# Fused retention and two MoE-style layers on one core: an early load of the first weight half, short tiles moved in the order of tiles, and their values loaded by two queues

## The chip, the cores and the metric

The kernel runs on one core of a Trainium2 chip. The metric is device time in microseconds (us) of one execution, as the median of several runs; lower is better. The trace shown is one execution, taken by the hardware profiler. Engines are PE (TensorE), DVE (VectorE), ACT (ScalarE), POOL (GpSimd) and SP (SyncE, which here only issues DMAs). ACT also issues DMAs, on a queue of its own.

## What is computed

Causal retention over 4 batches, 8 heads, 576 tokens and 64 channels a head, then two dense layers over the 2304 tokens, each with a weight into 2048 features, an elementwise function and a weight back to 512:

```python
scores = scale * np.matmul(q, k.transpose(0, 1, 3, 2))
gamma = 1.0 - 2.0 ** (-5.0 - np.arange(H, dtype=np.float32))
Dmat = np.where(rel >= 0, gamma[:, None, None] ** rel[None, :, :], 0.0)
x = np.matmul(scores * Dmat[None], v)          # then to (tokens, 512)
h = x @ w_in;   x = np.square(np.maximum(h, 0.0)) @ w_out
h = x @ w_in2;  out = (h * np.clip(h + 3.0, 0.0, 6.0) / 6.0) @ w_out2
```

All is float32; the weights come as 64-bit words that the kernel turns into float32 itself.

## The kernel before

**Retention, first 65 us.** The 576 tokens of a batch are cut into four full tiles of 128 and one short tile of 64. Batches are worked in pairs (0 and 1, then 2 and 3), and the list `tiles` (L199) holds 20 entries: for a pair, tile 0 of both batches, tile 1 of both, and so on, the two short tiles last. For tile `ti` the loop at the end of the file writes `stage_scores(ti)` (L302, matmuls `aps`; DVE multiplies them by a decay into `ret`, L310), then, for the tile before, `values(ti - 1)`: `stage_values` (L349, matmuls `vps` from `ret` and the values in `kvt`), `stage_state` (L325, `sps`, full tiles only), `stage_queries` (L361, into `vps` again, from the second tile of a batch on), DVE's copy into `xall` (L369) and ACT's copy of the state (L336, four instructions, full tiles only). POOL scales the keys of a full tile in place (L278). So PE's order for a full tile is scores of the next one, values, state, queries; a short tile has no state.

**Loads.** A full tile has two DMAs of 512 KB on SP: `qk` (L243) and `kv` (L257). Two short tiles of a pair form one unit: two DMAs of 256 KB for `qk` on SP (L248), and for the values two DMAs of 256 KB, one for each half of the partitions, both issued by ACT (L261). The first eight units are loaded at the start; the others as space comes free, from inside `values`. Eight semaphores are handed round to all DMAs of both queues in turn, so a DMA is issued when the one eight before it has landed, and an instruction behind it on its engine waits with it.

**Weights.** A weight half (chunk `c` of 128 features, `which` 0 for `w_in`, 1 for `w_out`) is loaded by `load_w` (for `w_in` of the first layer four DMAs, L137 to L141, in pieces of 1 KB; `w_out` one DMA, L145), then decoded: two ACT instructions (L165, L166), then DVE's (L169, L172, L178, L184), then `split_to` makes a high part on ACT (L190) and a low part on DVE or POOL (L191). The list `halves` is the order: (-2) `w_in` 0, (-2) `w_in` 1, (-1) `w_in` 2, (-1) `w_out` 0, then the rest. Before the change `w_in` 0 is loaded at `ti` 9 and `w_in` 1 at `ti` 13 (inside `values`), and five further halves at `ti` 14 to 18. `w_in` 0 is decoded from `ti` 14 on, `w_in` 1 after the last tile, `w_in` 2 and `w_out` 0 after the first chunk of the layer has been issued to PE.

**First layer.** For chunk `i`, `emit_h` issues 24 matmuls (`hps`, L434: 512 and 256 columns wide) into two banks that are the same for every one of the first 16 chunks; `emit_g` evacuates them with ACT (L454 to L456 on 512 columns, then on 256) and DVE (L460); `y_steps` of chunk `i - 2` follow (`yps`, L477). So the first three chunks, h0, h1 and h2, run with no `y` between them, and each needs the evacuation of the one before.

Of the kernel before, what the change touches and what calls it, by code (L numbers as in the profile page):

```python
# [24 lines left out]
C = 128  # L25
# [45 lines left out]
def retention_moe_moe2(ctx, tc, qk, qk_last, kv, w_in, w_out, w_in2, w_out2, consts, out):  # L71
# [127 lines left out]
    tiles = [(b, i, min(C, S - C * i)) for pair in range(0, B, 2) for i in range(NTB) for b in (pair, pair + 1)]  # L199
    data, rets, held = {}, {}, {}  # L200
# [22 lines left out]
    FULL = 2 * TILES  # L223
    UNITS = (FULL + 1) * (B // 2)

# [11 lines left out]
    def load_qk(u):  # L237
        p, i = divmod(u, FULL + 1)
        held[u] = spaces(u)
        first = (FULL + 2) * p + i  # L240
        if i < FULL:
            b, i, n = tiles[first]
            nc.sync.dma_start(out=held[u][0], in_=qk[b, i])  # L243
            data[first] = [held[u][0].rearrange("p (e a t) -> p e a t", e=2, a=HP)]
            return
        t = held[u][0].rearrange("p (b f) -> p b f", b=2)
        for k in range(2):
            nc.sync.dma_start(out=t[:, k], in_=qk_last[2 * p + k])  # L248
            data[first + k] = [t[:, k].rearrange("p (e a t) -> p e a t", e=2, a=HP)]

    def load_kv(u):
        p, i = divmod(u, FULL + 1)
        first = (FULL + 2) * p + i
        t = held.pop(u)[1].rearrange("p (e h d) -> p e h d", e=2, h=H)
        if i < FULL:
            b, i, n = tiles[first]
            nc.sync.dma_start(out=t, in_=kv[b, C * i:C * i + n])  # L257
            data[first] += [t[:, 0], t[:, 1]]
# [6 lines left out]
        for k in range(2):  # L265
            data[first + k] += [None, t[:, k]]
# [465 lines left out]
    with tc.manual_schedule():  # L732
# [6 lines left out]
        rows = place("t3", [128, C_END - C_GQ], F32, "rows")  # L739
# [3 lines left out]
        load_kv(1)  # L743
        for u in range(2, len(TOKENS) + WIDE):
            load_unit(u)
# [5 lines left out]
        def values(ti):  # L751
# [4 lines left out]
            u = ti // (FULL + 2) * (FULL + 1) + min(ti % (FULL + 2), FULL)  # L756
            if ti % (FULL + 2) == FULL:
                return
            if u < len(TOKENS):
                load_unit(u + len(TOKENS) + WIDE)  # L760
            elif len(TOKENS) + WIDE <= u < UNITS - len(TOKENS):
                load_unit(u + len(TOKENS))
            if ti in (9, 13):
# [6 lines left out]
        for ti in range(len(tiles)):  # L770
# [41 lines left out]
        due = [decode(*halves.pop(0)[1:])]  # L812
        due[0].pop(0)()
        for i, (pos, c) in enumerate(units):
            h = emit_h(pos, c)
            if i == 0:
                third_in, first_out = due.pop(0), decode(*halves.pop(0)[1:])
                third_in.pop(0)()
                split_in(0, 1, nc.vector)
                first_out.pop(0)()  # L820
                for f in third_in:
                    f()
                next_load()
                first_out.pop(0)()
                split_in(0, 2, nc.vector)
                for f in first_out:
                    f()
                next_load()
            dec, due = due, []
            for d in dec[:1]:  # L830
# [3 lines left out]
            for d in dec[1:]:  # L834
# [6 lines left out]
            for d in dec[1:]:  # L841
# [7 lines left out]
            if i and i + 2 < len(units):  # L849
# [127 lines left out]
```

## Time and profile before

| | |
|---|---|
| median of 3 runs | 850.76 us (849.04 to 851.12) |
| profiled execution, its own time | 849.55 us |
| its span | 847.8 us |
| PE busy in the span | 834.7 us (98%) |
| mean granted TensorE clock | 0.997 of full speed |
| DMA, mean over the span | 217 GB/s |

PE is nearly always busy, so the page's busy shares say little about one stage. The timeline names for each instruction the idle time before it and what ended that idle time; the chain of waits follows the end of the program back from step to step; the DMA view gives, for a stretch, what each queue moved. q1 is SP's data queue, q10 is ACT's, q8 and q14 bring instructions.

### The profile page before, as it was taken

Reading aid. Unit: us, or ns where it says so; the run is one execution under the profiler, and the core shown is the slowest. Engines: PE = TensorE matmul, PEld = TensorE weight load, DVE = VectorE, ACT = ScalarE, POOL = GpSimd, SP = SyncE. Lnnn points to the kernel's source line nnn. Section 1 sums busy time; section 2 is a strip of 40 time slices with the busy share of each in tenths; the row PEclk is TensorE's granted clock in tenths of the full one; section 3 lists DMA queues with packets and bytes.
Section 4 is the critical chain, followed back from the end, with each engine's and each line's share of the span. In section 5 each row is a group of like instructions: output and inputs, shape, how many; then the busy total and the mean of one; then the engine's idle time right before and its main releaser. Section 6 shows DMA issues by size and latency. Waiting matters only on the chain.

```text
span 847.8 us, 13400 instructions
## 1 busy us (share of the span) xinstructions
PE 834.7 (98%) x4964; PEld 724.2 (85%) x4964; DVE 526.4 (62%) x899; ACT 460.3 (54%) x879; POOL 134.9 (16%) x114
## 2 busy tenths in 40 slices
PE   8898999999999999999999999999999999999997
PEld 7887888888888888888888898989888898889886
DVE  5688777785676777787665544546654545634433
ACT  2248776776677777787765433344433335433332
POOL 3321333331332333242230000000000000000000
PEclk9999999999999999999999999999999999999999
DMA  9993656565678768876777464462764552864521
GB/s 335 354 308 109 187 190 183 191 190 198 215 270 302 258 243 277 307 262 242 268 245 264 165 222 185 151 226 95 277 256 163 176 210 87 308 225 162 202 97 74
DMA packets 67700, 183.95 MB, mean 217 GB/s; under 512 B 6834, under 2 KB 23346, under 8 KB 67636
## 3 DMA queue, kind: packets, MB, share of 16 engines
q1 hardware_dynamic: 66480, 181.17, 60.8%
q10 hardware_dynamic: 1156, 1.94, 0.8%
q8 instruction: 39, 0.64, 0.3%
q14 instruction: 25, 0.20, 0.1%
HBM read 146.90 MB, written 36.18 MB: 216 GB/s over the span
## 4 chain that ended last, share of the span: by engine, by line
PE 94%; DMA 4%; SPq 1%; DVE 0%; issue 0%; ACT 0%; ACTq 0%; DVEq 0%
PE yps L618 24%; PE hps L434 23%; PE yps L477 21%; PE hps L652 21%; PE ytail L477 3%; DMA early<-in_qk_dram 1%; PE aps L302 1%; PE vps L349 1%; DMA qkt<-in_qk_last_dram 1%; DMA qkt<-in_qk_dram 1%; PE vps L361 0%; PE sps L325 0%; DMA stage<-in_w_in_dram 0%; DVE w L184 0%; DVE a L178 0%
## 5 line engine op out<-in xcount | busy, mean ns | idle before, releaser
L618 PE MATMUL yps<-wo,g 128*128 128x512 f32 x864 | 226.4, 394 | 0.0
L477 PE MATMUL yps<-g,wo 128*128 128x512 f32 x768 | 195.3, 392 | 0.0
L618 PEld LDWEIGHTS yps<-wo,g 128*128 128x128 f32 x864 | 159.5, 188 | 23.9 <-DVE g L667 0.3
L477 PEld LDWEIGHTS yps<-g,wo 128*128 128x128 f32 x768 | 140.0, 188 | 27.5 <-POOL wo L191 3.1
L434 PE MATMUL hps<-xring,win 128*128 128x512 f32 (+1 forms) x720 | 155.0, 364 | 2.5 <-ACT r L454 2.5
L434 PEld LDWEIGHTS hps<-xring,win 128*128 128x128 f32 x720 | 124.3, 190 | 24.1 <-ACT r L454 2.7
L652 PE MATMUL hps<-xlast,win 128*128 128x384 f32 x576 | 116.1, 336 | 0.0
L652 PEld LDWEIGHTS hps<-xlast,win 128*128 128x128 f32 x576 | 103.2, 188 | 8.8
L671 DVE TENSOR_TENSOR u<-hps,u 128x384 f32<-128x384 f32 x48 | 26.8, 558 | 107.3 <-PE hps L652 107.3
L460 DVE TENSOR_TENSOR g<-r,g 128x512 fp32r<-128x512 f32 x64 | 47.6, 743 | 70.9 <-ACT g L456 70.5
L652 PE MATMUL hps<-xop,win 128*128 128x384 f32 x432 | 87.2, 336 | 0.0
L454 ACT ACTIVATE r<-hps 128x512 f32<-128x512 f32 x80 | 44.0, 549 | 73.9 <-PE hps L434 73.9
L665 ACT ACTIVATE g<-c 128x384 fp32r<-128x384 f32 x72 | 37.9, 526 | 84.3 <-DVE c L664 84.3
L652 PEld LDWEIGHTS hps<-xop,win 128*128 128x128 f32 x432 | 77.5, 188 | 6.6
L663 ACT ACTIVATE v<-c,three 128x384 f32<-128x384 f32 x72 | 44.5, 618 | 32.9 <-DVE c L671 31.6
L434 PE MATMUL hps<-xown,win 128*128 128x512 f32 x240 | 59.8, 390 | 0.7 <-ACT xall L486 0.7
L190 ACT ACTIVATE win<-w 128x512 fp32r<-128x512 f32 x64 | 39.7, 620 | 27.1 <-DVE w L184 27.1
L434 PEld LDWEIGHTS hps<-xown,win 128*128 128x128 f32 x240 | 44.8, 188 | 10.1 <-ACT xall L486 0.9
L690 ACT ACTIVATE c<-hps 128x384 f32<-128x384 f32 x24 | 11.8, 492 | 76.4 <-PE hps L652 76.4
L169 DVE TENSOR_SCALAR a<-a 128x512 f32<-128x512 f32 x64 | 38.5, 602 | 23.6 <-ACT a L165 23.6
L455 ACT ACTIVATE r<-r 128x512 f32<-128x512 f32 x80 | 47.2, 590 | 2.5
L664 DVE SCALAR_TENSOR_TENSOR c<-v,c 128x384 f32<-128x384 f32 x72 | 40.0, 555 | 13.7 <-ACT v L663 13.7
(90 smaller groups left out, 990.1 us busy)
## 6 DMA issues: line engine op xcount, KB each, us to landing
wo<-kept SPq DMA_DIRECT2D x96, 512.0 KB, 5.1
win<-kept SPq DMA_DIRECT2D x72, 512.0 KB, 3.6
kept<-ready SPq DMA_DIRECT2D x40, 512.0 KB, 3.7
stage<-in_w_out_dram SPq DMA_DIRECT2D x32, 512.0 KB, 4.1
kept<-wo SPq DMA_DIRECT2D x16, 512.0 KB, 5.0
stage<-in_w_in_dram SPq DMA_DIRECT2D x16, 512.0 KB, 4.0
qkt<-in_qk_dram SPq DMA_DIRECT2D x13, 512.0 KB, 6.9
kvt<-in_kv_dram SPq DMA_DIRECT2D x13, 512.0 KB, 7.9
```

Source lines behind the costliest of these rows:

```text
L169: nc.vector.tensor_scalar(out=a, in0=a, scalar1=LEAST, scalar2=MOST, op0=ALU.max, op1=ALU.min)
L190: lambda: nc.scalar.activation(out=hi, in_=src, func=ACTF.Copy),
L434: nc.tensor.matmul(out=h, lhsT=w[:, wp, kk * 128:kk * 128 + 128], rhs=xs[pos, kk][xp][:, o:o + n], start=m == 0, stop=m == 3 * KD - 1,)
L454: nc.scalar.activation(out=r, in_=hs[k], func=ACTF.Relu)
L455: nc.scalar.activation(out=r, in_=r, func=ACTF.Square)
L460: nc.vector.tensor_tensor(out=lo, in0=src, in1=hi.bitcast(F32), op=ALU.subtract)
L477: nc.tensor.matmul(out=p, lhsT=w[:, wp, m * 128:m * 128 + 128], rhs=g[pos, c][k][:, gpart, :size], start=c == 0 and e == 0 and not (k and ...
L618: nc.tensor.matmul(out=p, lhsT=gt[m // 3][:, gpart, m % 3 * 128:][:, :128], rhs=w[:, wp], start=first and e == 0, stop=last and e == 2,)
L652: nc.tensor.matmul(out=to, lhsT=wl[k][:, half, wp, o], rhs=x[:, xp, f], start=first and m == 0, stop=last and m == 5, skip_group_check=True,)
L663: nc.scalar.activation(out=v, in_=c, func=ACTF.Relu, bias=three)
L664: nc.vector.scalar_tensor_tensor(out=c, in0=v, scalar=6.0, in1=c, op0=ALU.min, op1=ALU.mult)
L665: nc.scalar.activation(out=hi, in_=c, func=ACTF.Copy)
```

## The change

- `load()` for `w_in` 0 is issued on SP right behind the loads of the first two tiles.
- The two short tiles of batches 0 and 1 move behind the first full tiles of batches 2 and 3; `groups` replaces the arithmetic on unit numbers. The short tiles of batches 2 and 3 stay last.
- Of the values of short tiles, the first half goes on SP with the other loads of the unit; the second half stays on ACT's queue, but is issued at `ti` 9 and `ti` 17.
- `w_in` 1 is loaded after tile 11, and is decoded from `ti` 16 on. `w_in` 0 is decoded from `ti` 2 on and split at `ti` 6; `w_in` 1 is split at the last tile. The block that was put into chunk 0 (`third_in`, `first_out`) is gone: `w_in` 2 and `w_out` 0 are decoded as any others, and `w_in` 2 is split after `emit_g` of chunk 0, low part on POOL.
- The constants' row tile `rows` moves from `t3` to `t6`, since `t3` now takes `w_in` 0.

```diff
-    tiles = [(b, i, min(C, S - C * i)) for pair in range(0, B, 2) for i in range(NTB) for b in (pair, pair + 1)]
-    data, rets, held = {}, {}, {}
+    steps = [(p, i) for p in range(B // 2) for i in range(TILES)]
+    for p in range(B // 2):
+        at = steps.index((p + 1, 0)) + 1 if 2 * p + 2 < B else len(steps)
+        steps.insert(at, (p, TILES))
+    tiles = [(2 * p + e, i, min(C, S - C * i)) for p, i in steps for e in range(2)]
+    groups = []
+    for ti, (b, i, n) in enumerate(tiles):
+        if n == C or b % 2 == 0:
+            groups.append((ti,) if n == C else (ti, ti + 1))
+    data, rets, held, other_half = {}, {}, {}, []
...
-        for e in range(2):
-            nc.scalar.dma_start(
+
+        def part(e, queue):
+            queue.dma_start(
                 out=t[half(e)].rearrange("p b h d -> p b (h d)"),
-                in_=kv[2 * p:2 * p + 2, C * TILES:, 1].rearrange("b t h d -> t b (h d)"),
+                in_=kv[b:b + 2, C * i:, 1].rearrange("b t h d -> t b (h d)"),
             )
-        for k in range(2):
-            data[first + k] += [None, t[:, k]]
+
+        part(0, nc.sync)
+        other_half.append(lambda: part(1, nc.scalar))
+        for k, ti in enumerate(groups[u]):
+            data[ti] += [None, t[:, k]]
...
-        rows = place("t3", [128, C_END - C_GQ], F32, "rows")
+        rows = place("t6", [128, C_END - C_GQ], F32, "rows")
         nc.scalar.dma_start(out=rows[:2], in_=consts[:2, C_GQ:])
         load = lambda: load_w(*coming.pop(0)[1:])
         load_kv(0)
         load_kv(1)
+        load()
...
-            if ti in (9, 13):
+            if ti == 11:
                 load()
...
             if len(tiles) - 6 <= ti < len(tiles) - 1:
                 load()
+            if ti in (9, 17):
+                other_half.pop()()
...
-            if 9 <= ti < 9 + KD:
-                high, low = split_x(0, ti - 9)
+            if 11 <= ti < 11 + KD:
+                high, low = split_x(0, ti - 11)
...
-            if ti == 14:
+            if ti in (2, 16):
                 decoding = decode(*halves.pop(0)[1:])
                 decoding.pop(0)()
-            if ti == 18:
+            if ti == 6:
                 split_in(0, 0, nc.gpsimd)
...
-        second_in = decode(*halves.pop(0)[1:])
-        second_in.pop(0)()
+            if ti == len(tiles) - 1:
+                split_in(0, 1, nc.gpsimd)
         values(len(tiles) - 1)
-        for f in second_in:
-            f()
-        next_load()
...
-        due = [decode(*halves.pop(0)[1:])]
-        due[0].pop(0)()
+        due = [decode(*halves.pop(0)[1:]) for _ in range(2)]
+        for d in due:
+            d.pop(0)()
...
-            if i == 0:
-                third_in, first_out = due.pop(0), decode(*halves.pop(0)[1:])
...
-                split_in(0, 2, nc.vector)
...
-            if i and i + 2 < len(units):
+            if i + 2 < len(units):
                 split_in(*units[i + 2], nc.gpsimd if i + 2 < NCH else nc.vector)
```

In the fences below each row is one instruction (or "xN" equal ones) as the engine gets it; the line numbers of the changed kernel are a few higher.

**First place: SP at the start of the program.** Before:

```order
L243 DMA qkt<-in_qk_dram 128x1024 x2
L257 DMA kvt<-in_kv_dram 128x1024 x2
L243 DMA qkt<-in_qk_dram 128x1024
L257 DMA kvt<-in_kv_dram 128x1024
L243 DMA qkt<-in_qk_dram 128x1024
L257 DMA kvt<-in_kv_dram 128x1024
```

and after the change:

```order
L246 DMA qkt<-in_qk_dram 128x1024 x2
L258 DMA kvt<-in_kv_dram 128x1024 x2
L137 DMA stage<-in_w_in_dram 128x2x128
L139 DMA stage<-in_w_in_dram 128x128
L140 DMA stage<-in_w_in_dram 64x128
L141 DMA stage<-in_w_in_dram 64x128
L246 DMA qkt<-in_qk_dram 128x1024
L258 DMA kvt<-in_kv_dram 128x1024
```

The four DMAs of `w_in` 0 stand ahead of the loads of the third tile and of all that follow.

**Second place: PE and ACT around the short tiles of batches 0 and 1, after the change.** PE, from the scores of tile 9 (a full one) on; `64x64` marks a short tile:

```order
L307 MATMUL aps<-qkt 128x128 x8
L354 MATMUL vps<-ret,kvt 64x128 x8
L330 MATMUL sps<-kvt 64x64 x8
L307 MATMUL aps<-qkt 64x64 x8
L354 MATMUL vps<-ret,kvt 64x128 x8
L330 MATMUL sps<-kvt 64x64 x8
L307 MATMUL aps<-qkt 64x64 x8
L354 MATMUL vps<-ret,kvt 64x64 x8
L366 MATMUL vps<-qkt,state 64x64 x8
```

ACT, from the first tiles on; the 12 state copies ahead of the DMA are those of tiles 6, 7 and 8, the four behind it those of tile 9:

```order
L341 ACTIVATE state<-sps,cst 128x64 x8
L165 ACTIVATE a<-stage 128x512
L166 ACTIVATE r<-stage 128x512
L341 ACTIVATE state<-sps,cst 128x64 x16
L190 ACTIVATE win<-w_255 128x512
L341 ACTIVATE state<-sps,cst 128x64 x12
L263 DMA kvt<-in_kv_dram 64x2x512
L341 ACTIVATE state<-sps,cst 128x64 x4
```

ACT before the change:

```order
L796 ACTIVATE cst<-gps 128x512
L336 ACTIVATE state<-sps,cst 128x64 x4
L261 DMA kvt<-in_kv_dram 64x2x512 x2
L336 ACTIVATE state<-sps,cst 128x64 x28
L190 ACTIVATE xring<-xall 128x768 x2
```

Both ACT loads stood behind the state copies of tile 0; the one that is left stands behind those of tile 8, and PE uses what it loads in the second `vps` row of a short tile (the row `L354 ... 64x64`), five rows of PE after the state of tile 8 (the first `sps` row).

**Third place: ACT between retention and the second evacuation.** After the change, from the high part of `w_in` 1 on:

```order
L190 ACTIVATE win<-w_255 128x512
L165 ACTIVATE a<-stage 128x512
L166 ACTIVATE r<-stage 128x512
L165 ACTIVATE a<-stage 128x512
L166 ACTIVATE r<-stage 128x512
L459 ACTIVATE r<-hps 128x512
L460 ACTIVATE r<-r 128x512
L461 ACTIVATE g<-r 128x512
L459 ACTIVATE r<-hps 128x256
L460 ACTIVATE r<-r 128x256
L461 ACTIVATE gtail<-r 128x256
L190 ACTIVATE win<-w_1093 128x512
```

Then come one high part (`wo`), two decode instructions and the evacuation of h1. Before the change:

```order
L190 ACTIVATE win<-w_822 128x512
L165 ACTIVATE a<-stage 128x512
L166 ACTIVATE r<-stage 128x512
L165 ACTIVATE a<-stage 128x512
L166 ACTIVATE r<-stage 128x512
L190 ACTIVATE win<-w_822 128x512
L165 ACTIVATE a<-stage 128x512
L166 ACTIVATE r<-stage 128x512
L190 ACTIVATE win<-w_1090 128x512
L454 ACTIVATE r<-hps 128x512
```

The first evacuation (`r<-hps`) stood behind the high parts of `w_in` 1 and `w_in` 2, which wait for DVE; now it stands behind four decode instructions only, and the high part of `w_in` 2 comes behind it.

## Rows read from the trace of the kernel before

**Rows 1.** Page, part 1: busy us, share of the span, instructions by engine

```profile
PE 834.7 (98%) x4964; PEld 724.2 (85%) x4964; DVE 526.4 (62%) x899; ACT 460.3 (54%) x879; POOL 134.9 (16%) x114
```

**Rows 2.** Waits of PE, 0 to 110 us: us in total, times, longest

```profile
PE vps L349 <- issue: 1.7, 1, 1.7
PE vps L349 <- DVE xall L369: 0.5, 1, 0.5
```

**Rows 3.** Timeline, start: start us, us, engine, operation, idle before and releaser

```profile
10.65 1.16 PE L302 MATMUL aps<-qkt 64*128 64x128 f32 x16
10.85 0.69 ACTq L261 DMA_DIRECT2D kvt<-in_kv_dram  x1
11.40 1.04 POOL L278 TENSOR_TENSOR kvt<-kvt,cst 128x512 f32<-128x512 f32 x1 [1.52 <-DMA kvt<-in_kv_dram]
...
13.96 1.04 POOL L278 TENSOR_TENSOR kvt<-kvt,cst 128x512 f32<-128x512 f32 x1 [1.52 <-DMA kvt<-in_kv_dram]
...
21.62 1.16 PE L302 MATMUL aps<-early 64*128 64x128 f32 x16 [1.96 <-DMA early<-in_qk_dram]
```

**Rows 4.** Chain of waits in order of time: start us, us on the chain, what

```profile
24.86 1.09 PE aps L302 x16
25.96 1.02 PE vps L349 x16
26.98 0.46 PE sps L325 x16
27.45 0.60 PE vps L361 x16
...
34.33 0.39 PE aps L302 x14
...
38.69 0.23 PE vps L361 x16
...
86.12 4.18 PE hps L434 x24
```

**Rows 5.** DMA view, 35 to 39 us: packets, MB, share of 16 engines

```profile
q8 instruction: 1, 0.02, 1.7%
```

**Rows 6.** DMA view, 58.2 to 61 us (a `w_in` half in flight)

```profile
q1 hardware_dynamic: 854, 0.79, 105.2%
```

**Rows 7.** DMA view, 11.6 to 14.3 us: the only data queue with packets

```profile
q1 hardware_dynamic: 304, 1.11, 102.3%
```

**Rows 8.** DMA view, 14.5 to 20 us

```profile
q10 hardware_dynamic: 279, 0.52, 33.0%
```

**Rows 9.** Line L261, the four ACT loads of short values, from issue to landing

```profile
DMA to landing us min/median/max: 8.3/8.6/10.1
```

**Rows 10.** Page, part 6: KB each, median us from issue to landing

```profile
win<-kept SPq DMA_DIRECT2D x72, 512.0 KB, 3.6
```

**Rows 11.** Timeline, end of retention to the first layer

```profile
62.69 0.27 PE L349 MATMUL vps<-ret,kvt 64*64 64x64 f32 x2
...
64.76 4.45 PE L434 MATMUL hps<-xring,win 128*128 128x512 f32 x24
...
71.70 10.21 PE L434 MATMUL hps<-xring,win 128*128 128x512 f32 x48 [2.50 <-ACT r L454]
...
81.75 0.86 PE L477 MATMUL yps<-g,wo 128*128 128x512 f32 x3
```

**Rows 12.** Busy time by stretch: us, engines busy, PEclk (granted clock), DMA share, GB/s

```profile
71.70:75.40 3.70, 3.70 (x9) 2.94 (x10) 3.21 (x7) 3.60 (x8) 0.00 (x0) 0.54 0.02 4
```

**Rows 13.** Groups by form, 0 to 85 us: busy us, mean ns, idle before

```profile
L165 ACT ACTIVATE a<-stage 128x512 f32<-128x512 f32 x7 | 4.7, 670 | 0.6 <-issue 0.6
...
L184 DVE CUSTOM_DVE_ANT_0 w<-a,r 128x1024 uint16<-128x1024 uint16 x4 | 2.8, 690 | 0.3
...
L190 ACT ACTIVATE win<-w 128x512 fp32r<-128x512 f32 x4 | 2.5, 632 | 3.0 <-DVE w L184 3.0
...
L454 ACT ACTIVATE r<-hps 128x512 f32<-128x512 f32 x3 | 1.8, 587 | 0.5 <-PE hps L434 0.5
```

More of the change, by code (lines that the diff above doesn't have):

```diff
@@ L221, in make_last_decay @@
             )
-    FULL = 2 * TILES
-    UNITS = (FULL + 1) * (B // 2)
     wide = []
@@ L237, in load_qk @@
     def load_qk(u):
[L238 removed]
         held[u] = spaces(u)
[L240 to L242 removed]
+        b, i, n = tiles[groups[u][0]]
+        if n == C:
             nc.sync.dma_start(out=held[u][0], in_=qk[b, i])
[L244 removed]
+            data[groups[u][0]] = [held[u][0].rearrange("p (e a t) -> p e a t", e=2, a=HP)]
             return
         t = held[u][0].rearrange("p (b f) -> p b f", b=2)
[L247 to L249 removed]
+        for k, ti in enumerate(groups[u]):
+            nc.sync.dma_start(out=t[:, k], in_=qk_last[b + k])
+            data[ti] = [t[:, k].rearrange("p (e a t) -> p e a t", e=2, a=HP)]
     def load_kv(u):
[L252 to L253 removed]
+        b, i, n = tiles[groups[u][0]]
         t = held.pop(u)[1].rearrange("p (e h d) -> p e h d", e=2, h=H)
[L255 to L256 removed]
+        if n == C:
             nc.sync.dma_start(out=t, in_=kv[b, C * i:C * i + n])
[L258 removed]
+            data[groups[u][0]] += [t[:, 0], t[:, 1]]
             return
[L260 to L261 removed]
+        def part(e, queue):
+            queue.dma_start(
                 out=t[half(e)].rearrange("p b h d -> p b (h d)"),
[L263 removed]
+                in_=kv[b:b + 2, C * i:, 1].rearrange("b t h d -> t b (h d)"),
             )
[L265 to L266 removed]
+        part(0, nc.sync)
+        other_half.append(lambda: part(1, nc.scalar))
+        for k, ti in enumerate(groups[u]):
+            data[ti] += [None, t[:, k]]
     def load_unit(u):
@@ L755, in values @@
             stage_state_copy(ti)
-            u = ti // (FULL + 2) * (FULL + 1) + min(ti % (FULL + 2), FULL)
-            if ti % (FULL + 2) == FULL:
+            u = next(u for u, g in enumerate(groups) if ti in g)
+            if ti != groups[u][-1]:
                 return
@@ L811, in retention_moe_moe2 @@
         sums, highs, lows = operand_steps(0)
-        due = [decode(*halves.pop(0)[1:])]
-        due[0].pop(0)()
+        due = [decode(*halves.pop(0)[1:]) for _ in range(2)]
+        for d in due:
+            d.pop(0)()
         for i, (pos, c) in enumerate(units):
             h = emit_h(pos, c)
-            if i == 0:
-                third_in, first_out = due.pop(0), decode(*halves.pop(0)[1:])
[L818 to L824, printed above, removed]
-                split_in(0, 2, nc.vector)
-                for f in first_out:
-                    f()
-                next_load()
             dec, due = due, []
-            for d in dec[:1]:
+            first = dec if i == 0 else dec[:1]
+            dec = dec[len(first):]
+            for d in first:
                 for f in d:
@@ L833, in retention_moe_moe2 @@
                 next_load()
-            for d in dec[1:]:
+            for d in dec:
                 d.pop(0)()
@@ L840, in retention_moe_moe2 @@
             emit_g(pos, c, h)
-            for d in dec[1:]:
+            for d in dec:
                 for f in d:
```

2 lines of the change are left out of this document (1 added, 1 removed).

## The prediction

> **What bounds the kernel now.** I read the page first: PE is busy 834.7 of 847.8 us [rows 1], so only idle PE and PE at the lower clock can be won or lost. The waits of PE and the timeline then show where it idles in the first 85 us: 1.96 us before the scores of the sixth tile, which wait for a load [rows 3]; 0.5 us and 1.7 us around the first short tiles [rows 2]; and 2.50 us between h0 and h1, ended by ACT's evacuation [rows 11]. After that last gap the granted clock is 0.54 of full over 3.7 us [rows 12], that is the 1.2 GHz level for some 3.4 us, and h1 with h2 take 10.21 us [rows 11] where two later chunks take 2 x 4.18 [rows 4]: 1.85 us more. From the first `y` step at 81.75 on [rows 11] the work is the same in both kernels and PE-bound. So the forecast is the shift of that moment. The last values of retention that two kernels can be compared by are the first short tile's of batches 2 and 3, at 62.69 [rows 11]; from there to the `y` step before the change are 19.06 us.
>
> **Step 1, the early half.** `w_in` 0 comes in front of the third tile. At full rate a 512 KB DMA takes 1.28 us: one tile is two of them, and the keys of two tiles start 2.56 us apart [rows 3]. In 1 KB pieces the queue moved 0.79 MB in 2.8 us [rows 6], so 0.52 MB is 1.86 us; bounds 1.28 and 2.1, I take 1.86. The third tile's keys started on landing at 11.40, its first DMA one place earlier at about 10.1 [rows 3]; both come 1.86 later, so its scores start at 12.0, not 10.65. From there PE goes on without waiting: a tile is 1.09 + 1.02 + 0.46 + 0.60 = 3.17 us, 2.57 without queries [rows 4], so the sixth tile's scores start at 12.0 + 2.57 + 2 x 3.17 = 20.9. Its load would land near 13.9 + 1.86 + 3 x 1.28 = 19.6: in front of it the two ACT loads are gone, which had stretched those three DMAs from 3.84 to 7.6 us (13.9 to 21.5) [rows 3]. Instead of 21.62 it is 20.9: **-0.7**. DVE's and ACT's decode of this half moves to a place where the same engines have the same work a tile; I cost it at nothing, as it cost PE nothing at tiles 14 to 17; without that cover it is four DVE steps of at most 0.7 each [rows 13].
>
> **Step 2, the short tiles in another place.** The 0.5 us (PE was ahead of DVE's copy) and the 1.7 us with no releaser [rows 2] belonged to two short tiles behind each other. In the second, one 16 KB transfer of instructions falls in the stretch [rows 5]; I read it as PE short of instructions, because short tiles use them up fastest. Now full-width work lies between the short scores, the same number of instructions takes some 1.4 us longer (0.39 for short scores against 1.09, twice [rows 4]), and I keep 0.3 of the 2.2: **-1.9**; bounds -2.2 and 0. The Trainium skill ("Runtime: NRT & Kernel Launch", Instruction fetch mechanics) has the crossing of such a block mostly hidden; by that the gap has another cause and may stay, and the sum would be 1.7 higher. The 1.70 us in the trace speaks against "hidden" here.
>
> **Step 3, the second half of the first short values.** This is the new wait. ACT's load was issued at 10.85, just after the first state [rows 3], and used 23 us later. Now it is issued after the state of tile 8, and PE gets to its use after short scores, values, state, short scores: 0.39 + 1.02 + 0.46 + 0.39 = 2.26 us [rows 4], 2.4 with what is left of the 0.5. The four such loads took at least 8.3 us to land [rows 9]. The nearest for below are SP's loads in quiet stretches, 3.6 us for twice the bytes [rows 10]. Here the queue is not quiet: SP issues its loads until the semaphore ring stops it, eight DMAs ahead. Before, in 11.6 to 14.3 only SP's queue had packets, though ACT's load had been issued at 10.85 [rows 3, 7]; in 14.5 to 20 both ACT loads passed, 0.52 MB in 5.5 us [rows 8]. So: about 3.4 us before the first packet, 2.75 for one load, 0.4 for the last engine: 6.6 from issue, nearest to the 8.3 row but with one load instead of two. State 8 ends 5.74 us after the scores of tile 8 begin (two scores, two values, two states, one queries). Those begin three tiles of 3.17 after the sixth, at 30.4; so issue 36.2, landing 42.8, use at 38.5: **+4.3**; bounds +1.0 and +5.9. Queued behind on PE is everything; behind on SP the reload of that unit's space, which has five tiles of slack.
>
> A gap that long is beyond the 2.50 us after which the clock fell, while 1.96 and 1.70 did not lower it. So the clock falls: **+1.5** (1.85 was the price in wide matmuls).
>
> **Step 4, the second half of the last short values.** Issue after state 16, use after queries, short scores, a full values-state-queries, short scores: 0.60 + 0.39 + 1.02 + 0.46 + 0.60 + 0.39 = 3.46, less 0.1. On SP the five weight halves are in flight then, mostly landed; I take 5.4 us: **+2.0**; bounds 0.2 and 5.2.
>
> **Step 5, the first layer's start.** From the values of the first last short tile the path is now ACT's: short matmuls, DVE's copy and last decode step (about 1.8 us, L184 0.69 [rows 13]); then sixteen ACT instructions up to and with the evacuation of h1, thirteen at 0.59 to 0.67 and three half as wide, 9.5 us [rows 13]; then h2, 4.18 [rows 4]. That is 15.5, with latencies 15.8, against 19.06: **-3.3**. Below stands the path of PE alone, 1.0 + 3 x 4.18 = 13.5 (-5.5), above 16.7 (-2.4). The 2.50 us gap goes, and with it the lower clock. POOL's low part of `w_in` 2 and the decode on DVE end before h2 is free; if they did not, h2 would wait for them.
>
> **Sum.** -0.7 - 1.9 + 4.3 + 1.5 + 2.0 - 3.3 = +1.9 us on the profiled 849.55, which lies 1.2 below the median of the runs; on the median of 850.76 it gives 852.7. A measurement of this kernel can tell about 0.3% from no change, 2.5 us; so the forecast is **no change**, a little to the slow side, of itself 850.5 to 855.
>
> **Rivals.** *Faster: the ACT loads land soon.* If ACT's queue is served at once beside SP's, a load lands after about 4.0 us, the 3.6 of quiet stretches [rows 10] and 0.4 for the last engine: step 3 is 36.2 + 4.0 - 38.5 = 1.7 and too short for the clock, step 4 is 0.6. Sum -0.7 - 1.9 + 1.7 + 0.6 - 3.3 = -3.6: 847.2; with no wait at all 844.9. For it: only one load at a time now. Against: the stretch with SP's packets alone [rows 7]. The Trainium skill ("DMA: Bandwidth & Descriptors", Queues, rings and completion order) has each DMA engine go round the queues that have work, packet by packet, which is this rival; by that rule the time is this one. The trace agrees once both have packets [rows 8], not for the three us before [rows 7].
>
> *Slower: both loads take what they took before.* With 8.3 and 8.6 us [rows 9] step 3 is 6.0 and step 4 5.2, and the clock falls twice (the second time partly under ACT's path, 0.7): -0.7 - 1.9 + 6.0 + 1.5 + 5.2 + 0.7 - 3.3 = +7.5: 858.3. It decides from a landing of 7.3 us on in both places. For it: the shortest of four was 8.3. Against: those came in pairs.
>
> *Short waits, smaller gain.* The gap of 1.7 us stays and step 5 gives 2.4 only, with waits as in the first rival: -0.7 - 0.2 + 1.7 + 0.6 - 2.4 = -1.0: 849.8.
>
> That the change does not do what it says is excluded by the order of instructions.
>
> **How the numbers follow.** Forecast 0.52, of it 0.36 within 0.3% and 0.16 above, since its upper end is past 853.3. Fast landing 0.20, all faster. Old landing 0.20, all slower. The last one 0.08: 0.04 same, 0.02 to each side. Faster 0.22, same 0.40, slower 0.38. The range takes in both outer cases without their far ends: 846.0 to 858.0.
>
> **What would show it.** Right: in PE's waits two new rows at the line of the short values, ended by the DMA of the values, near 38.5 to 43 and near 65, with the clock lower after the first; no gap above 1 us between h0 and h1 and full clock there; no wait at the sixth tile, one of about 1.3 us at the third. From issue to landing ACT's two loads at 5 to 7 us. Wrong: these loads landing within 3 us of use, or the wait between h0 and h1 still above 2 us, or a PE waiting for loads at the fourth or fifth tile.

## The result, and the profile after

The changed kernel takes 859.13 us in the median (858.90 to 861.59), the kernel before, run beside it, 850.07 us (849.04 to 851.12). The ratio is 1.0113 with an interval of 1.0096 to 1.0131: slower by 9 us, above the stated range of 846 to 858 us. The profiled execution took 858.92 us, its span is 857.1 us against 847.8.

Page, part 1, of the changed kernel: PE is as busy as before to 0.4% [rows 1]. The 9.3 us are idle time and time at the lower clock.

```profile
PE 837.8 (98%) x4964; PEld 726.7 (85%) x4964; DVE 526.5 (61%) x897; ACT 459.8 (54%) x879; POOL 136.2 (16%) x116
```

Waits of PE over the whole span (us in total, times, longest). The first row was not there before [rows 2]. The gap without a releaser is still 1.7 us.

```profile
PE vps L354 <- DMA kvt<-in_kv_dram: 7.9, 2, 4.0
PE aps L307 <- DMA qkt<-in_qk_dram: 3.1, 3, 2.5
PE vps L354 <- issue: 1.7, 1, 1.7
...
PE hps L439 <- ACT r L459: 0.2, 1, 0.2
```

Timeline of PE (start us, us, idle before and releaser). It answers to [rows 3, 11]: third and sixth tile, the first short values, two tiles after them, the last short values, h0 with h1, h2, and the first `y` step.

```profile
12.50 1.16 PE L307 MATMUL aps<-qkt 64*128 64x128 f32 x16 [2.52 <-DMA qkt<-in_qk_dram]
...
21.68 1.16 PE L307 MATMUL aps<-early 64*128 64x128 f32 x16
...
40.31 0.33 PE L354 MATMUL vps<-ret,kvt 128*64 128x128 f32 x2 [1.74 <-issue]
...
41.65 0.28 PE L354 MATMUL vps<-ret,kvt 64*64 64x64 f32 x2
45.83 0.59 PE L354 MATMUL vps<-ret,kvt 64*64 64x64 f32 x11 [3.90 <-DMA kvt<-in_kv_dram]
...
46.89 2.08 PE L307 MATMUL aps<-qkt 64*128 64x128 f32 x16
...
51.96 1.13 PE L354 MATMUL vps<-ret,kvt 128*64 128x128 f32 x16
...
69.68 0.22 PE L354 MATMUL vps<-ret,kvt 64*64 64x64 f32 x1
...
73.99 0.59 PE L354 MATMUL vps<-ret,kvt 64*64 64x64 f32 x11 [4.03 <-DMA kvt<-in_kv_dram]
...
75.90 10.23 PE L439 MATMUL hps<-xring,win 128*128 128x512 f32 x48
86.36 4.49 PE L439 MATMUL hps<-xring,win 128*128 128x512 f32 x24 [0.23 <-ACT r L459]
90.69 0.63 PE L482 MATMUL yps<-g,wo 128*128 128x512 f32 x2
```

Busy time by stretch (us; busy PE, PEld, DVE, ACT, POOL; granted clock; DMA share; GB/s). The clock was 0.50, the 1.2 GHz level, from the start of the first wait (41.9) on and from within the second (69.96 to 73.99) on; between these stretches and after them it was full. Scores that take 1.16 us take 2.08 at 46.89.

```profile
41.90:52.00 10.10, 6.20 (x97) 5.52 (x96) 3.83 (x9) 1.92 (x4) 3.12 (x3) 0.50 0.60 195
52.20:72.40 20.20, 17.76 (x386) 15.97 (x382) 16.49 (x32) 8.17 (x28) 2.09 (x2) 1.00 0.98 295
72.60:79.30 6.70, 5.31 (x70) 4.54 (x71) 3.26 (x8) 2.90 (x5) 1.29 (x1) 0.50 0.02 7
```

The first `y` step is 8.94 us later than before (90.69 against 81.75), and that is nearly all of the 9.3. The rest is mostly a wait of 0.28 us in the next `y` step, for a `w_out` half from POOL.

### The profile page after: what moved, and what is told of

Same layout as the page of the kernel before. It is cut to its first block, busy times and chain, and to the rows that moved or that the text cites. A ratio compares the mean times of both kernels' runs of the same rounds, so it can differ in the third digit from the quotient of the medians.

```text
span 857.1 us, 13416 instructions
## 1 busy us (share of the span) xinstructions
PE 837.8 (98%) x4964; PEld 726.7 (85%) x4964; DVE 526.5 (61%) x897; ACT 459.8 (54%) x879; POOL 136.2 (16%) x116
## 4 chain that ended last, share of the span: by engine, by line
PE 92%; DMA 5%; ACT 2%; issue 0%; POOL 0%; DVE 0%; SPq 0%; ACTq 0%; DVEq 0%
PE yps L623 23%; PE hps L439 22%; PE hps L657 21%; PE yps L482 20%; PE ytail L482 2%; DMA stage<-in_w_in_dram 2%; DMA kvt<-in_kv_dram 2%; PE aps L307 1%; PE vps L354 1%; DMA qkt<-in_qk_dram 1%; DMA qkt<-in_qk_last_dram 1%; PE vps L366 1%; PE sps L330 0%; ACT r L460 0%; ACT r L459 0%
## 5 line engine op out<-in xcount | busy, mean ns | idle before, releaser
L439 PEld LDWEIGHTS hps<-xring,win 128*128 128x128 f32 x720 | 124.3, 190 | 21.9 <-ACT r L459 0.4
L668 ACT ACTIVATE v<-c,three 128x384 f32<-128x384 f32 x72 | 44.4, 617 | 32.9 <-DVE c L676 31.7
L439 PEld LDWEIGHTS hps<-xown,win 128*128 128x128 f32 x240 | 44.8, 188 | 10.1 <-ACT xall L491 0.9
```

The lines of the kernel that those rows point to most:

```text
L439: nc.tensor.matmul(out=h, lhsT=w[:, wp, kk * 128:kk * 128 + 128], rhs=xs[pos, kk][xp][:, o:o + n], start=m == 0, stop=m == 3 * KD - 1,)
L668: nc.scalar.activation(out=v, in_=c, func=ACTF.Relu, bias=three)
```

## The experiments

Every ratio is to the kernel before on the same chip. A kernel with one time only has no ratio. Waits and starts are those of its profiled execution.

### Both halves of the short values on SP

```diff
-        other_half.append(lambda: part(1, nc.scalar))
+        part(1, nc.sync)
...
-            if ti in (9, 17):
+            if False:
```

> The changed kernel with one edit: the second half of the short values is issued by SP right behind the first, with the other loads of the unit, so some 10 us and 12 us before its use. Late-issue theory (the two waits of 3.90 and 4.03 us at the short values, and the lower clock behind each, are the loss): both waits go and the clock stays full, 3.9 + 2.9 + 4.0 + 1.6 us less than the changed kernel's profiled 858.9, so 846.5 us, between 845 and 849, faster than both kernels. Rival, supply theory (DMA data as a whole comes later in the changed kernel, and the short values are only where it shows): PE waits elsewhere instead and the time stays within 852 to 858.

Measured: 851.69 us, ratio 1.0006 (0.9995 to 1.0018). No wait for `kvt` is left, and the first `y` step stands at 82.97. So ACT's second halves, with all that follows from them, cost nearly all of it: 1.0113 less 1.0006 is 9.1 of 9.6 us. But the time is that of the kernel before, not the 845 to 849 us expected: in this trace PE's gaps without a releaser come to 4.3 us (1.7 before the change), the longest 2.59 (to 40.77), with the clock at 0.50 from 40.5 to 43.7.

### ACT's loads two tiles earlier, and one tile earlier

```diff
-            if ti in (9, 17):
+            if ti in (7, 15):
```

> The changed kernel with the ACT loads issued at ti 7 and 15 in place of 9 and 17, two full tiles or 6.3 us earlier; the queue stays ACT's. Late-issue theory: landing 8 to 9 us after issue lies before the use, no wait at the short values, full clock, time equal to the kernel with both halves on SP within 1.5 us (845 to 850). Queue theory (a load on ACT's queue is always served last and stretches SP's loads): the waits stay at 2 us or more, or a new wait of PE for an SP load of 2 us or more appears, and the time stays above 851.

Measured: 851.15 us, ratio 0.9998 (0.9987 to 1.0010); the profiled execution, at 849.78 the fastest of the ten, had full clock throughout. The loads took 10.1 and 6.6 us to land, longer than in the changed kernel, and nobody waited for them. So the fault is the place of their issue, not ACT's queue as such. The time is above the 845 to 850 expected. With `(8, 16)` instead:

> ACT loads at ti 8 and 16, one full tile or 3.17 us earlier than in the change. Late-issue theory: the first wait falls from 3.90 to about 0.7 us; the second, which I put down to ACT's issue waiting for a semaphore slot until the fourth weight half had landed, falls to under 1 us, since at ti 16 its slot is that of an older load; clock stays full; time about 847 to 850. Supply theory: the waits keep their length within 1 us, time above 855.

Measured: 853.03 us (one run). The waits for `kvt` were still 1.34 and 2.62 us, where about 0.7 and under 1 were expected. Two tiles are enough, one is not. The second load was held by an older DMA, as it had been by a younger one in the changed kernel (step 4 below): ACT came to it at 59.3 and stood 2.9 us at its semaphore, which by the program's list of instructions is that of the first piece of `w_in` 2. SP had issued that piece at 54.99, it took 7.2 us to land (62.2), and ACT issued at 62.25. ACT's lines for the load, and the landing of that piece (line L137):

```profile
L263 ACTq EVENT_SEMAPHORE  x1: 2909/2909/2909, 59.3 to 59.3; - x1
```

```profile
DMA to landing us min/median/max: 7.2/7.2/7.2
```

The timeline of the first of these two, with loads two tiles earlier, is the undisturbed form of the change, and I use it below as the measure: third tile, short values, two tiles, last short values, h0 with h1, h2, `y`.

```profile
12.30 1.16 PE L307 MATMUL aps<-qkt 64*128 64x128 f32 x16 [2.68 <-DMA qkt<-in_qk_dram]
...
39.66 0.33 PE L354 MATMUL vps<-ret,kvt 128*64 128x128 f32 x2 [1.17 <-issue]
...
41.00 0.56 PE L354 MATMUL vps<-ret,kvt 64*64 64x64 f32 x13
...
46.13 0.60 PE L307 MATMUL aps<-qkt 64*128 64x128 f32 x6 [1.69 <-issue]
46.66 1.09 PE L354 MATMUL vps<-ret,kvt 128*64 128x128 f32 x16
...
65.21 0.27 PE L354 MATMUL vps<-ret,kvt 64*64 64x64 f32 x3
...
66.97 8.64 PE L439 MATMUL hps<-xring,win 128*128 128x512 f32 x48
76.57 4.45 PE L439 MATMUL hps<-xring,win 128*128 128x512 f32 x24 [0.96 <-ACT r L459]
80.85 0.86 PE L482 MATMUL yps<-g,wo 128*128 128x512 f32 x3
```

### Eight fewer warm-up matmuls

```diff
-WARM = 18
+WARM = 10
```

> The changed kernel with 10 warm-up matmuls at the start in place of 18, so that each later PE instruction stands 16 places earlier in PE's stream. Instruction-supply theory of the 1.7 us gap without a releaser: the gap stays about 1.7 us but lies 8 matmuls later in the program, so in the state matmuls of tile 9 (or the scores of the second short tile) and no longer at the 14th matmul of the values of tile 9. Rival (a hidden wait on another engine or bank): the gap stays at the 14th matmul of the values of tile 9. Time: within 2 us of the changed kernel either way, unless the gap goes.

Measured: 859.11 us (one run), as the changed kernel. The gap without a releaser moved from the values of tile 9 into the state matmuls behind them, eight matmuls later, and became shorter. The wait for the first short values became longer, 4.67 us where it was 3.90:

```profile
40.35 0.56 PE L330 MATMUL sps<-kvt 128*64 128x64 f32 x11 [0.68 <-issue]
...
46.30 0.59 PE L354 MATMUL vps<-ret,kvt 64*64 64x64 f32 x11 [4.67 <-DMA kvt<-in_kv_dram]
```

So this gap belongs to a place in PE's stream of instructions and not to a tile: shown. And here a shorter gap only made the wait for the load behind it longer; the time stayed.

### The early half behind the sixth unit

Base: ACT's loads two tiles earlier.

```diff
         load_kv(1)
-        load()
         for u in range(2, len(TOKENS) + WIDE):
+            if u == 6:
+                load()
             load_unit(u)
...
-            if ti in (2, 16):
+            if ti in (6, 16):
...
-            if ti == 6:
+            if ti == 10:
                 split_in(0, 0, nc.gpsimd)
```

> The kernel with ACT's loads two tiles earlier, with w_in 0 loaded behind the sixth unit instead of behind the second, decoded from tile 6 and split at tile 10. If the early half only delays the third tile's load by its own bytes and that wait (2.68 us of PE at 12.30 in the run before this one) never comes back, the wait at the third tile falls to below 0.5 us, no other wait for a load grows above 0.5, and the time is 2 to 2.5 us below the other's: ratio to the kernel before about 0.997. If all the loads together are the limit of the first 20 us, the same bytes make a later tile wait instead: 1.5 to 2.7 us before the scores of the sixth to eighth tile, and ratio 0.9995 to 1.001.

Measured: 850.66 us, ratio 0.9996 (0.9987 to 1.0005). The wait at the third tile fell to 0.4 us, as expected. But 0.57 us for DVE and 0.74 for a load came later, and the gap of 1.17 at the same place of the stream became 2.54. The wait went and nothing was won; neither theory had the gap.

```profile
39.91 0.33 PE L354 MATMUL vps<-ret,kvt 128*64 128x128 f32 x2 [2.54 <-issue]
```

### The short tiles back in their place

Base: ACT's loads two tiles earlier (the first one moves with the short tiles).

```diff
-        at = steps.index((p + 1, 0)) + 1 if 2 * p + 2 < B else len(steps)
+        at = steps.index((p + 1, 0)) if 2 * p + 2 < B else len(steps)
...
-            if ti in (7, 15):
+            if ti in (5, 15):
```

> The kernel with ACT's loads two tiles earlier, with the short tiles of the first pair back behind the fourth full tiles of their own pair; all else as there. If the gaps that end in 'issue' belong to PE's instructions as they are laid out and to no tile, some of them stay, at other matmuls, 2 to 3.5 us in all, and the time is within 1 us of the kernel before (ratio 0.999 to 1.001): the move of the short tiles is worth nothing. If the move made or prolonged them, they fall to the 2.2 us of the kernel before and the time falls by 1.3 us: ratio 0.998. If the move saves what step 2 said (1.9), the time rises by 1.5 to 2: ratio 1.002.

Measured: 850.25 us, ratio 0.9996 (0.9985 to 1.0007). The gaps sum to 3.0 us, nearly all in one of 2.70 at another instruction. The move of the short tiles is worth nothing that can be measured.

```profile
35.68 1.09 PE L354 MATMUL vps<-ret,early 128*64 128x128 f32 x16 [2.70 <-issue]
```

### The early half alone

The kernel before, with this only:

```diff
+        load()
         for u in range(2, len(TOKENS) + WIDE):
...
-            if ti in (9, 13):
+            if ti == 13:
```

(The row tile `rows` moves to `t6`, as in the change.)

> The kernel before with w_in 0 loaded behind the first two tiles, and nothing else. By step 1 of the prediction the third tile starts 1.3 us later and the sixth 0.7 earlier: 850.4 to 850.8, ratio 0.999. By the trace of the changed kernel the sixth tile starts where it did, so the early half gains nothing: ratio 1.000. With ACT's two loads still on the way beside it, the 0.52 MB more may make the sixth tile wait longer instead: up to 1.3 us, ratio 1.0015; and if the wait at the third tile lowers the clock, up to 1.5 more, ratio 1.003.

Measured: 853.62 us, ratio 1.0034 (1.0022 to 1.0046). It costs 2.7 us, the last of the three expectations. In place of one wait of 1.96 us [rows 3] there are three, and behind the last the clock is 0.54 in 21.9 to 25.3.

```profile
12.55 1.16 PE L302 MATMUL aps<-qkt 64*128 64x128 f32 x16 [2.48 <-DMA qkt<-in_qk_dram]
...
16.43 1.16 PE L302 MATMUL aps<-qkt 64*128 64x128 f32 x16 [1.23 <-DMA qkt<-in_qk_dram]
...
21.94 1.89 PE L302 MATMUL aps<-qkt 64*128 64x128 f32 x16 [2.26 <-DMA qkt<-in_qk_dram]
```

### The first layer's start alone

The kernel before, with `w_in` 0 and 1 loaded and decoded within retention and the block in chunk 0 gone:

```diff
-            if ti in (9, 13):
+            if ti in (4, 9):
                 load()
...
-            if ti == 14:
+            if ti in (10, 16):
                 decoding = decode(*halves.pop(0)[1:])
                 decoding.pop(0)()
-            if ti == 18:
+            if ti == 15:
                 split_in(0, 0, nc.gpsimd)
...
+            if ti == len(tiles) - 1:
+                split_in(0, 1, nc.gpsimd)
```

(The rest of it, from `second_in` down, is as in the change.)

> The kernel before with only the part on the start of the first layer: w_in 0 loaded after tile 4 and w_in 1 after tile 9, both decoded within retention, the block in chunk 0 gone. Order of tiles and ACT's loads as before. If the start of the first layer is worth what the trace of the changed kernels shows (13.9 us from h0 to the first y step instead of 17.0) and nothing in retention pays for it, the time is 2.5 to 3.3 us below the kernel before: 848 to 849, ratio 0.9962 to 0.997, with full clock between h0 and h2. If the gain needs the short tiles moved or the load at the start, ACT or DVE is late at h0 instead, by 1.5 to 3 us, and the ratio is 0.999 to 1.001.

Measured: 849.58 us, ratio 0.9987 (0.9977 to 0.9997). h0 to the first `y` step takes 13.92 us (65.82 to 79.74) where it took 16.99 [rows 11], at full clock, as expected. But the ratio lies between the two expectations: the first `y` step is only 2.0 us earlier than before, since h0 comes later, and of these 0.6 went one chunk later:

```profile
64.74 0.86 PE L349 MATMUL vps<-ret,kvt 64*64 64x64 f32 x13 [0.85 <-DVE ret L310]
...
65.82 8.62 PE L434 MATMUL hps<-xring,win 128*128 128x512 f32 x48
...
79.74 0.86 PE L477 MATMUL yps<-g,wo 128*128 128x512 f32 x3
...
89.32 0.50 PE L477 MATMUL yps<-g,wo 128*128 128x512 f32 x1 [0.57 <-POOL wo L191]
```

### The same, with `w_out` 1 on DVE: the best version

```diff
-            if ti in (10, 16):
+            if ti in (10, 15):
...
-                split_out(max(i - 1, 0), nc.vector if i == 0 else nc.gpsimd)
+                split_out(max(i - 1, 0), nc.vector if i in (0, 2) else nc.gpsimd)
```

> The kernel with only the part on the first layer's start, and two things that its trace showed late: the low part of w_out 1 on DVE instead of POOL (a wait of 0.57 us of PE in the y step of the second chunk), and w_in 1 decoded one tile earlier (0.85 us of PE before the last short values, behind DVE's decode). If the gain at the first y step (2.0 us earlier than in the kernel before) was given back because w_out 1 was late there, the wait goes and 0.6 to 1.2 us more are won: 848.4 to 849, ratio about 0.998. If it is given back by the work of the chunks as such, the wait turns up at another tile of the same stretch and the time stays within 0.3 us of the other: ratio 0.9985 to 0.999.

Measured: 848.69 us, ratio 0.9977 (0.9967 to 0.9986). The wait for `w_out` 1 is gone, and the one of h2 for ACT is 0.26 us instead of 0.97. The wait of 0.85 behind DVE's decode stayed. Two things were changed at once, and the interval overlaps with that of the version before, so what `w_out` 1 alone is worth in time is not shown. This version is faster than the kernel before by some 2 us, and than the changed one by 11.

### The same, with the short values on SP, or issued at tile 4

```diff
-            nc.scalar.dma_start(
+            nc.sync.dma_start(
                 out=t[half(e)].rearrange("p b h d -> p b (h d)"),
```

> The same kernel, with both halves of the short values issued on SP, in the order of the units, instead of on ACT's queue; no early half, short tiles where the kernel before has them. If ACT's two loads are what delays the loads of the fifth to eighth tile (2.6 us of PE's waits for qkt and early in the run with the first layer's part alone), those waits fall below 1 us and the time falls by 1 to 2 us: ratio 0.996 to 0.997. If the loads in sum set the time there, or PE's gaps for instructions grow by what the loads' waits lose, the time stays: ratio 0.998 to 0.999, with the same sum of waits under other names.

Measured: 849.66 us, ratio 0.9989 (0.9981 to 0.9998). The waits for `qkt` and `early` fell from 2.3 us to 0.4, and the time rose by 1: one gap of 2.69 us, and the clock behind it at 0.61 for 3.4 us.

```profile
32.19 1.29 PE L349 MATMUL vps<-ret,early 128*64 128x128 f32 x16 [2.69 <-issue]
```

```profile
29.50:32.10 2.60, 0.01 (x1) 0.07 (x1) 1.10 (x4) 0.00 (x0) 0.00 (x0) 1.00 1.02 364
32.20:35.60 3.40, 3.40 (x56) 3.28 (x57) 0.16 (x1) 0.93 (x4) 1.04 (x1) 0.61 1.02 406
```

In the second kernel ACT's two loads of the first short values come at tile 4 instead of behind the first state:

```diff
+            if ti == 4:
+                later.pop()()
```

> The kernel with the first layer's part, w_out 1 on DVE and w_in 1 decoded one tile earlier, and both of ACT's loads for the first short values issued at tile 4 (about 20 us) instead of behind the first state. If those two loads delay the loads of the fourth to sixth tile and nothing takes the place of the waits, these fall from 2.3 us to below 1 and the time by 1 to 1.5 us: ratio 0.996 to 0.9965. If PE only comes sooner to the place where it lacks instructions, the gap that ends in 'issue' grows from 1.7 to about 2.7 us there, and the ratio is 0.997 to 0.998, as without it; a gap above 2.5 us with the lower clock behind it would cost 1 us more: 0.998 to 0.999.

Measured: 848.85 us, ratio 0.9982 (0.9973 to 0.9991). The waits for loads fell to 0.4 us here too, and the gap stayed at 1.7. A third thing took their place, which I had not expected: DVE. Waits of the values for `ret`, 0.9 us in the version before, are now 3.3. The longest of them, 1.32, may have two causes: it ends at 31.43, but DVE's step ended at 30.98, and a 16 KB transfer of instructions had begun 2.4 us before (29.01), as at the gaps of the last section.

```profile
PE vps L352 <- DVE ret L313: 3.3, 6, 1.3
PE vps L352 <- issue: 1.7, 1, 1.7
```

### Another semaphore for ACT's second load

```diff
-    stagep = pool("stage", 3)
+    stagep = pool("stage", 2)
```

> The changed kernel with two stage buffers in place of three, so that w_in 4's four DMAs are issued only when w_in 3 is decoded; ACT's second load then comes four places earlier in the ring and has the semaphore of an older DMA. If the semaphore held ACT's second load in the changed kernel (issued at 69.29, at once after the DMA that used its semaphore before had landed at 69.2, though the state copy of tile 16 had begun at 66.37), it is issued 2 to 3 us earlier relative to that copy, lands 4.5 to 5.5 us later, and PE's second wait for the short values falls from 4.03 to 1.3 to 2.3 us. If ACT's own work or the queue held it, issue and wait stay as they were, at about 3 us behind the copy and 4 us. The total may be longer by a late w_in 4 at the chunk that needs it, which is looked at apart.

Measured: 927.1 us (one run), which says nothing on the question: with two buffers the weights come late through both layers (PE waits 20.6 us for `wo` alone). The place itself answers it. Timeline of ACT in this kernel:

```profile
66.74 0.93 ACT L341 ACTIVATE state<-sps,cst 128x64 f32<-128x64 f32 x4 [1.11 <-PE sps L330]
67.64 0.61 ACTq L263 DMA_DIRECT2D kvt<-in_kv_dram  x1
```

The load is issued 0.90 us behind the start of the state copy, where it was 2.92 in the changed kernel (below). It lands 4.3 us later, at 71.9, and PE's wait at this place is 1.75 us instead of 4.03, within the 1.3 to 2.3 expected:

```profile
71.07 0.86 DVE L315 TENSOR_TENSOR ret<-aps,decay_last 64x256 f32<-64x256 f32 x2
```

```profile
72.08 0.40 PE L354 MATMUL vps<-ret,kvt 64*64 64x64 f32 x11 [1.75 <-DVE ret L315]
```

The view puts this wait down to DVE's `ret`, which ended at 71.93, at the same moment as the load landed; but these are the values of the first short tile, and that `ret` belongs to the second. `w_in` 4's 0.5 MB were not in flight beside the load, but the landing is only 0.3 us shorter for that. That the semaphore held the load back is shown.

## Why the prediction was wrong

The direction on its slow side was right, the size was not. Of the signs that the prediction named, the two new waits at the short values came, but the third tile waited 2.52 us and not about 1.3, and the landings of 8.4 and 4.6 us both lay outside 5 to 7. The same cuts through both traces, each a difference to the kernel before:

| step | predicted | measured |
|---|---|---|
| 1, early half (sixth tile at 21.68, was 21.62) | -0.7 | +0.06 |
| 2, short tiles moved (21.68 to 51.96, was 21.62 to 45.11; less the next two) | -1.9 | +0.45 |
| 3, wait for the first short values | +4.3 | +3.90 |
| 3, clock behind it | +1.5 | +2.44 |
| between (51.96 to 69.68, was 45.11 to 62.69) | 0 | +0.14 |
| 4, wait for the last short values | +2.0 | +4.03 |
| 4, clock behind it | 0 | +1.34 |
| 5, first layer's start, undisturbed | -3.3 | -3.42 |
| sum, first `y` step | +1.9 | +8.94 |

The undisturbed values are those of the run with ACT's loads two tiles earlier. From the first short values to the values two tiles on it takes 46.66 - 41.00 - 1.69 = 3.97 us, the changed kernel 51.96 - 41.65 - 3.90 = 6.41: 2.44 for the clock. From the last short values to `y` it takes 80.85 - 65.21 = 15.64, the changed kernel 90.69 - 69.68 - 4.03 = 16.98: 1.34 for the clock, and 15.64 against 19.06 is step 5. The cut at 45.11 in the kernel before:

```profile
45.11 1.09 PE L349 MATMUL vps<-ret,kvt 128*64 128x128 f32 x16
```

**Step 1 failed.** I let the sixth tile gain because ACT's two loads no longer stood in front of it. Its wait of 1.96 us did go, but it came at 21.68, not 20.9: the third tile came at 12.50 instead of the 12.0 of the sum, the fifth tile waited 0.18 for its load, and the tiles between took 0.1 more. So the size of the wait at the third tile was wrong, and the gain was too small to bear it. Alone, beside ACT's loads, the early half costs 2.7 us; put behind the sixth unit its wait goes, and the gap for instructions grows from 1.17 to 2.54. The cover that I named for DVE's decode held: PE waited for no decode in retention.

**Step 2 failed.** I read the 1.7 us gap rightly as PE short of instructions, and wrongly as belonging to short tiles. It stands at a place in the stream: eight warm-up matmuls fewer moved it by eight matmuls. It stayed, at 1.74 in the changed kernel, and the moved tiles need about 0.9 us more for the same work (21.60 to 46.66 in the undisturbed form, less its gaps of 1.17 and 1.69, is 22.20 us; 21.62 to 45.11 before, less 0.51 and 1.70, is 21.28). The rule of the Trainium skill that spoke against this step ("Runtime: NRT & Kernel Launch", Instruction fetch mechanics: crossing a block of instructions is mostly hidden) would have had the gap stay for another cause. It stayed; but that it is an instruction gap, not hidden, is what the moved warm-up shows.

**Step 3 held in size, by two errors that cancel.** The load was issued at 37.32, not 36.2, and landed 8.4 us later, not 6.6 (line L263, the stretch from 37 to 38 us):

```profile
DMA to landing us min/median/max: 8.4/8.4/8.4
```

Its use was later too, at 41.7 instead of 38.5, above all since the gap of step 2 stayed in front of it. So the values of steps 2 and 3 trade against each other: with eight fewer warm-up matmuls the gap was 0.68 and the wait 4.67. Of the terms of the 6.6, the 0.4 us for the last engine stood on no row; here the last two of the sixteen updates of the load's semaphore come 0.6 us apart (45.12 and 45.69). The first three us of the landing went as I had read it from [rows 7]: from 37.3 to 40.3 only SP's queue had packets.

```profile
q1 hardware_dynamic: 324, 1.18, 99.1%
```

In 37.3 to 41.8 ACT's queue moved 0.07 MB, in 41.8 to 45.8, with SP's share down to 83%, 0.19. The rival in which the load lands soon, with the rule of the Trainium skill behind it ("DMA: Bandwidth & Descriptors", Queues, rings and completion order), fell here: taking turns packet by packet is not what the first three us show, and even after them ACT's queue had 19% of the engines' time beside SP's 83. Whether its descriptors were not yet there, or were there and not served, no run here separates.

**The clock was sized too small.** I took 1.5 us from the gap of 2.50 before [rows 11, 12], where the clock was low for some 3.4 us. With the wait of 3.90 us it was low for 10.1 us, of which 3.9 are the wait itself, and with the second, which I gave no price at all in the forecast, for 6.7, of which 1.4 are the wait. The price does not follow from the length of the wait: with eight fewer warm-up matmuls the wait of 4.67 us had the clock low for 6.7 us (44.4 to 51.1). Nor does the reading hold that 1.96 us is too short for a fall and 2.50 is long enough: with the loads two tiles earlier the clock stayed full behind 2.68 us at the third tile (above), and with the loads one tile earlier it was 0.50 from 12.3 to 15.6, behind 1.94 us at the same tile:

```profile
11.92 1.81 PE L307 MATMUL aps<-qkt 64*128 64x128 f32 x16 [1.94 <-DMA qkt<-in_qk_dram]
```

**Step 4 is the main miss.** With the clock behind it, it is 3.4 of the 7.0 us between sum and measurement (step 2 is 2.35). Its 2.0 took the issue to follow the state copy of tile 16, the weight halves to be mostly landed, and the landing to take 5.4 us. The landing was shorter, 4.6. The issue was late, and the halves had not landed: SP was still issuing the last of them from 66.82 to 69.64. In the program's list of instructions the load waits for the semaphore that the second piece of `w_in` 3 has (each DMA waits for the one that had its semaphore last; between these two lines stand seven others, four of them those of `w_in` 4):

```
L139 DMA stage<-in_w_in_dram 128x128 [waits DMAHW7_49]
L263 DMA kvt<-in_kv_dram 64x2x512 [waits DMAHW7_49,Pool_49]
```

Timeline of SP and of ACT in the changed kernel, the state copy of tile 16 and the load:

```profile
63.84 0.33 SPq L139 DMA_DIRECT2D stage<-in_w_in_dram  x1
```

```profile
66.37 0.93 ACT L341 ACTIVATE state<-sps,cst 128x64 f32<-128x64 f32 x4 [1.11 <-PE sps L330]
69.29 0.61 ACTq L263 DMA_DIRECT2D kvt<-in_kv_dram  x1
70.00 0.93 ACT L341 ACTIVATE state<-sps,cst 128x64 f32<-128x64 f32 x4 [2.71 <-PE aps L307]
```

That piece took 5.4 us to land (63.84 + 5.4 = 69.2), and ACT issued at 69.29. The text ahead of the prediction says that a DMA is issued when the one eight before it has landed; step 3 used it for SP, and step 4 did not ask which DMA that is for ACT's own. With an older DMA in that place the load went out 2.0 us sooner behind the copy, and the wait for it fell to 1.75 us. The rival *Slower* (858.3) came nearest to the time, with both loads landing in over 8 us and the clock falling twice; only the first did so, and the second wait had the semaphore as its cause.

**Step 5 held.** -3.42 where nothing disturbs it, against -3.3, on the path that was named: ACT's chain up to the evacuation of h1. But it arrives in the time only in part. Put alone into the kernel before, h0 came 1.06 us later than there (65.82 against 64.76), 0.85 of it behind DVE's decode of `w_in` 1; so the first `y` step was 2.0 us earlier, and the runs by 1.1. 0.57 us in between went to `w_out` 1, whose low part POOL made late: with that part on DVE the wait is gone. The ratio goes from 0.9987 to 0.9977, which the intervals do not separate.

**Why the undisturbed change only ties.** With ACT's loads in time h0 comes 2.2 us later than before (66.97 against 64.76). Of these 0.9 are the moved short tiles, 0.65 the gaps up to 46.66 (1.17 and 1.69, where 0.51 and 1.70 were), 0.65 a new gap for instructions at the last short scores. The first `y` step is then 0.9 us earlier, and 0.6 of that goes in the next one, to POOL. Taking a part out of the change (the early half, the short tiles) did not free this sum: a longer gap for instructions or a wait for DVE stood in its place each time. Why such a gap is as long as it is in a given version is not explained; that stays open.

## What to carry to other kernels

Before a late load is costed by its landing time, look up which DMA its semaphore waits for: where queues share their semaphores, as here, a load that is issued "just in time" behind a burst on another queue waits for that burst, and its issuing engine with it. A wait of PE has to be priced with the clock behind it, and as a range: here the clock added 3.8 us to 7.9 us of waits, and nothing to one of 2.68. And a gain near the start of a PE-bound program counts only as far as the next late thing (a load, a DVE step, PE's instructions): follow the first instruction of each stage, not the wait that went.

## What the runs showed of the hardware that was not expected

- PE's gaps without a releaser end a nearly fixed time after a 16 KB transfer of instructions begins: 36.04 to 38.43 before, 37.83 to 40.31 in the changed kernel, 29.51 to 32.19 with all short values on SP. Over the 22 such gaps of the first 95 us in the fourteen traces here it is 2.3 to 2.8 us, of which the packet itself takes 1.1 to 1.3. By this reading the gap is what PE has not covered of that time, 0.3 to 2.7 us.
- Most such transfers cost nothing, and which of them does changes from version to version: with the same order of instructions on PE, the gap stood behind the transfer at 36.23 in the best version and behind the one before it, at 29.51, with the short values on SP.
- A load of 256 KB on ACT's queue landed in 4.3 us where SP's queue had 47% of the DMA engines' time meanwhile (the run with another semaphore), and in 10.1 us where it had 95% (the run with loads two tiles earlier, 31 to 41 us). These are two places with other loads beside them, and no run changes the share alone.
- ACT stood at the semaphore of another queue's DMA three times, and each time issued within 0.1 us of that DMA's landing: at 69.29 in the changed kernel, at 62.25 with the loads one tile earlier, and at 67.64 with another semaphore (60.49 + 7.1 = 67.6, the third piece of `w_in` 2 by the program's list).
